# Sliding-window attention and gated FFN on one core: DMA transposes and loads one group earlier, batch 3 on the steady pattern

## The chip, the cores and the metric

The kernel runs on one core of one Trainium2 chip. Times are device microseconds (us) of a whole execution. The kernel before took 365.98 us (median of 6 runs beside the changed one; 365.95 in the three runs from which the prediction starts). The profile's span starts at the first instruction and ends at the last one, and is some 1.75 us shorter than the measured time. Names of engines are those of the profile: PE is TensorE (matmuls), ACT is ScalarE, DVE is VectorE, POOL is GpSimd (here it issues the loads), and SP issues the other transfers from its queue.

## The reference

```python
scores = scale * np.matmul(q, k.transpose(0, 1, 3, 2))      # 8 batches, 8 heads, 576 x 64
mask = (rel >= 0) & (rel < 128)                             # causal window of 128
scores = np.where(mask, scores + bias, -1e9)                # ALiBi bias
attn = softmax(scores)
x = np.matmul(attn, v)  ->  (4608 tokens, 512)
g, val = x @ w_gate, x @ w_val                              # 512 -> 1536
out = (gelu(g) * val) @ w_out                               # 1536 -> 512
```

## The kernel before

The FFN runs in nine groups of 512 tokens. A group is twelve gate blocks (`gate_val`, eight 512-column matmuls each) and eight output halves (`out_half`, six matmuls each). The attention of later batches is woven in between. For each batch there are scores (PE), exps (ACT), a mask product (DVE), row sums (PE), reciprocals (DVE), the spread of the reciprocals over 128 partitions, and values (PE) with a product into `xT` (DVE). The spread is done in two ways: by PE with copies on ACT and DVE, or through DRAM by DMA.

```python
    def transposes_dma(b):                      # q and k of batch b, SBUF to SBUF, on the SP queue
        for src, dst in ((ks, kT), (qs, qT)):
            nc.sync.dma_start_transpose(...)

    def spread_dma(b):                          # 18 KB to DRAM, then two broadcast reads
        d = d_pool.tile([4, 2, S], FP32, name="rd")
        nc.sync.dma_start(out=d.rearrange("c i s -> (c i) s"), in_=sumrow[b][0:128:16, :])
        for i in (0, 1):
            nc.sync.dma_start(out=recip[b][64 * i:64 * i + 64, :, :],
                              in_=d[:, i, :].unsqueeze(0).to_broadcast((64, 4, S)))

    def spread_pe(b, s):                        # four fp32 matmuls (eight records), four copies
        ...

    def finish(b, s):
        spread_pe(b, s)
        values(b, s, range(4))

    todo = {                                    # what stands between the output halves 0 to 7 of a group
        ...
        2: [("s", 3, 1, (0, 1), lambda: sums(3, 0)), 0, ("s", 3, 1, (2, 3)), 1,
            ("finish", 3, 0), ("s2", 4), ("sum", 3, 1), 2,
            ("s", 4, 0, (0, 1)), 3, ("finish", 3, 1), 4, ("s", 4, 0, (2, 3)), 5,
            ("s", 4, 1, (0, 1)), 6, 7, ("s", 4, 1, (2, 3))],
    }
```

`("s", b, s, cs)` is a lot of scores, 8 matmuls where `s` is 0 and 12 where it is 1, into four PSUM banks (PSUM is the memory that takes PE's results; `ps` in the traces). `("s2", b)` is the diagonal block of all heads, two banks. Tiles of PSUM come from eight banks, which are reused in the order in which the program frees them.

The softmax here doesn't subtract the row's maximum and nothing guards it: scores larger than these inputs give would overflow.

Of the kernel before, what the change touches and what calls it, by code (L numbers as in the profile page):

```python
# [26 lines left out]
def kernel(  # L27
# [11 lines left out]
    B, H, S, D = q.shape  # L39
# [27 lines left out]
    def bank():  # L67
        ps = psum.tile([128, 512], FP32, name="ps")
        for _ in range(heat.pop()):
            nc.tensor.matmul(out=ps, lhsT=zeros[:, 0:128], rhs=zeros, start=True, stop=True)  # L70
        heat.append(0)
        return ps
# [19 lines left out]
    def load(t, src, b, js=range(5)):  # L92
        for j in js:
            lo = 64 if j == 0 else 0
            nc.gpsimd.dma_start(  # L95
                out=t[lo:128, j, :].rearrange("p (h d) -> p h d", h=H),
                in_=src[b][:, 128 * j - 64 + lo:128 * j + 64, :].rearrange("h p d -> p h d"))

    def load_qk(b):
        load(qs[b % 2], q, b)  # L100
        load(ks[b % 2], k, b)
# [18 lines left out]
    def load_v(b, js=range(5)):  # L120
        load(vb[b % 2], v, b, js)
# [34 lines left out]
    def transpose(b, what, c, copy):  # L156
        ps = bank().bitcast(BF16)
        for j in range(5):
            nc.tensor.transpose(  # L159
                out=ps[:, 128 * j:128 * j + 128],  # L160
                in_=(qs, ks)[what][b][:, j, 128 * c:128 * c + 128], identity=ident)
        copy(out=(qT, kT)[what][b][:, :, c, :],
             in_=ps[:, 0:640].rearrange("p (j t) -> p j t", t=128))
# [7 lines left out]
    def transposes_dma(b):  # L171
        for src, dst in ((ks, kT), (qs, qT)):
            nc.sync.dma_start_transpose(
                out=dst[b % 2].rearrange("p j c t -> p (j c) t"),
                in_=src[b % 2].rearrange("p j x -> p (j x)"))
# [53 lines left out]
    def prob(b, s, c, i, j, n):  # L229
        if (s, j) == (0, 2):  # L230
            return probs2[b][:, c, i, 0:n]
        return probs[b, s, c][:, i, PCOL[s][j]:PCOL[s][j] + n]
# [3 lines left out]
    def sums(b, s):  # L236

        ps = bank()
        for j, a, e in PIECES[s]:
            for i in (0, 1):  # L240
                for c in range(4):
                    nc.tensor.matmul(  # L242
                        out=ps[32 * c:32 * c + 32, a:e],
                        lhsT=ones[:, min(j, 1), i, :], rhs=prob(b, s, c, i, j, e - a),
                        start=(i == 0 and j == 2 * s), stop=(i == 1 and j == 2 * s + 2),
                        skip_group_check=True)
        if b not in sumrow:
            sumrow[b] = r_pool.tile([128, S], FP32, name="r")
            recip[b] = r_pool.tile([128, 4, S], FP32, name="rb")
        lo, hi = PART[s]  # L250
        nc.vector.reciprocal(sumrow[b][:, lo:hi], ps[:, 0:hi - lo])  # L251

    def spread_dma(b):
# [3 lines that stand above are left out]
            nc.sync.dma_start(  # L257
                out=recip[b][64 * i:64 * i + 64, :, :],
                in_=d[:, i, :].unsqueeze(0).to_broadcast((64, 4, S)))
# [14 lines left out]
    def values(b, s, cs):  # L274
        lo, hi = PART[s]
        pss = []
        for c in cs:
            ps = bank()
            pss.append(ps)
            for j, a, e in PIECES[s]:  # L280
                for i in (0, 1):
                    h = 2 * c + i
                    nc.tensor.matmul(  # L283
                        out=ps[64 * i:64 * i + 64, a:e],
                        lhsT=vb[b % 2][:, j, 64 * h:64 * h + 64],
                        rhs=prob(b, s, c, i, j, e - a),
                        start=(j == 2 * s), stop=(j == 2 * s + 2), skip_group_check=True)
        for c, ps in zip(cs, pss):
            nc.vector.tensor_tensor(  # L289
                out=xT[:, c, b * S + lo:b * S + hi], in0=ps[:, 0:hi - lo],  # L290
                in1=recip[b][:, c, lo:hi], op=ALU.mult)
# [7 lines left out]
    def gate_val(g, f, lo=0, hi=512, later=None):  # L299
        if g not in hid:  # L300
            hid[g] = h_pool.tile([128, NF, 512], BF16, name="hT")
        t0 = 512 * g
        pg, pv = bank(), bank()
        for w, ps in ((wg, pg), (wv, pv)):
            for c in range(4):
                nc.tensor.matmul(  # L306
                    out=ps[:, 0:hi - lo], lhsT=w[:, c, 128 * f:128 * (f + 1)],
                    rhs=xT[:, c, t0 + lo:t0 + hi], start=(c == 0), stop=(c == 3))

        def act():  # L310
            gl = g_pool.tile([128, 512], BF16, name="gelu")
            nc.scalar.activation(out=gl[:, 0:hi - lo], in_=pg[:, 0:hi - lo], func=AF.Gelu)  # L312
            nc.vector.tensor_tensor(out=hid[g][:, f, lo:hi], in0=pv[:, 0:hi - lo],  # L313
                                    in1=gl[:, 0:hi - lo], op=ALU.mult)

        if later is None:
            act()
        else:
            later.append(act)
# [3 lines left out]
    def out_half(g, u):  # L323
        t, half = u // 2, u % 2
        if half == 0:
            acc[g] = bank()
        po = acc[g]
        for f in range(6 * half, 6 * half + 6):
            nc.tensor.matmul(  # L329
                out=po, lhsT=hid[g][:, f, 128 * t:128 * (t + 1)],  # L330
                rhs=wo[:, f, :], start=(f == 0), stop=(f == NF - 1))
        if half == 1:
            osb = o_pool.tile([128, DM], FP32, name="osb")
            nc.scalar.copy(out=osb, in_=po)  # L334
            r0 = 512 * g + 128 * t
            nc.sync.dma_start(out=out[r0:r0 + 128, :], in_=osb)
# [103 lines left out]
    for t in (qs[0], ks[0]):  # L440
# [10 lines left out]
        1: [("s2", 2), ("s", 2, 0, (0, 1)), 0, ("s", 2, 0, (2, 3)), 1, 2,  # L451
            ("s", 2, 1, (0, 1), lambda: sums(2, 0)), 3, ("s", 2, 1, (2, 3)), ("s2", 3),
            ("finish", 2, 0), 4, ("sum", 2, 1), ("s", 3, 0, (0, 1)), 5, 6,
            ("finish", 2, 1), ("s", 3, 0, (2, 3)), 7],
        2: [("s", 3, 1, (0, 1), lambda: sums(3, 0)), 0, ("s", 3, 1, (2, 3)), 1,
            ("finish", 3, 0), ("s2", 4), ("sum", 3, 1), 2,
            ("s", 4, 0, (0, 1)), 3, ("finish", 3, 1), 4, ("s", 4, 0, (2, 3)), 5,
            ("s", 4, 1, (0, 1)), 6, 7, ("s", 4, 1, (2, 3))],
    }

    def steps(g):
        b = g + 2
        if g in todo:
            return todo[g]
        if b >= B:
            return range(8)
        return [("s2", b), ("s", b, 0, (0, 1)), 0, 1, ("s", b, 0, (2, 3)), 2, 3,
                ("s", b, 1, (0, 1)), 4, 5, ("s", b, 1, (2, 3)), 6, 7]

    RUN = {"s2": scores2, "s": scores, "sum": sums, "finish": finish}  # L470

    for g in range(NG):
        for b in ((), (2, 3), (4,))[g] if g < 3 else ():
            transposes_dma(b)
        if g + 2 < B:
            load_v(g + 2)
        for f in range(6 if g == 0 else 0, NF):
            gate_val(g, f)
            if g == 0 and f >= 8:
                for w in (0, 1):  # L480
                    transpose(1, w, f - 8, (act, dve)[w])
            if 3 <= g < B - 1:
                if f == 0:
                    sums(g + 1, 0)
                    sums(g + 1, 1)
                    spread_dma(g + 1)
                    if g + 2 < B:
                        transposes_dma(g + 2)
                elif f in (8, 10):
                    for s in (0, 1):  # L490
                        values(g + 1, s, (f - 8, f - 7))
        if g + 3 < B:
            load_qk(g + 3)
        for item in steps(g):
            if isinstance(item, int):
                out_half(g, item)
            else:
                RUN[item[0]](*item[1:])

# [29 lines left out]
```

## Time and profile before

| | before |
|---|---|
| median time | 365.98 us |
| span of the profile | 364.2 us |
| PE busy | 352.5 us, 97% |
| DVE, ACT busy | 52%, 51% |
| groups 1, 2, 3, 4 | 42.52, 40.21, 37.99, 37.40 us |

The last row is the measure. It is the distance from the first gate row of a group to the first gate row of the next one in the timeline of PE. Groups 4 and 5 have the steady pattern.

### The profile page before, as it was taken

The numbers are of one execution on the slowest core, as the hardware profiler recorded it, in microseconds if no ns is written. First come the engines' busy times: TensorE is split into PE (matmuls) and PEld (weight loads), VectorE is DVE, ScalarE is ACT, GpSimd is POOL, SyncE is SP. The second block draws the span as 40 slices with busy tenths as digits, with TensorE's granted clock in tenths as the row PEclk, the third lists the DMA queues.
The fourth block names the chain that finished last, engine by engine and source line by source line (L and its number), as shares of the span: only waits on it lengthen the run. The fifth ranks groups of instructions, "written<-read, shape, count | busy, mean of one in ns | idle before, by whom it ended". The sixth has DMA issues, their size and how long they took to land.

```text
span 364.2 us, 6748 instructions
## 1 busy us (share of the span) xinstructions
PE 352.5 (97%) x2702; PEld 172.1 (47%) x2702; DVE 189.4 (52%) x308; ACT 187.5 (51%) x340; POOL 109.1 (30%) x140
## 2 busy tenths in 40 slices
PE   7899999999999999999999999999999999999995
PEld 2467545444454445444444444444444444444442
DVE  4876458533795369484537554745465404302320
ACT  5963486435956376933883278336842223313321
POOL 8966769912629103900940040000000000000000
PEclk9999999999999999999999999999999999999999
DMA  9999999999979985999991992093205030011002
GB/s 105 161 193 175 172 161 185 183 147 193 178 100 131 153 67 83 164 101 218 117 213 42 199 112 88 35 200 71 88 33 130 2 115 0 4 58 58 2 29 86
DMA packets 151168, 41.41 MB, mean 114 GB/s; under 512 B 138816, under 2 KB 144448, under 8 KB 151136
## 3 DMA queue, kind: packets, MB, share of 16 engines
q0 software_dynamic: 112608, 18.88, 67.9%
q1 hardware_dynamic: 38528, 22.10, 27.7%
q8 instruction: 21, 0.34, 0.4%
q14 instruction: 11, 0.09, 0.1%
HBM read 42.47 MB, written 9.51 MB: 143 GB/s over the span
## 4 chain that ended last, share of the span: by engine, by line
PE 86%; ACT 5%; DMA 2%; POOL 2%; DVE 2%; issue 1%; POOLq 0%; DVEq 0%; ACTq 0%
PE ps L306 51%; PE ps L329 24%; PE ps L283 4%; ACT P L187 4%; PE ps L180 3%; DMA vb<-in_v_dram 2%; PE ps L242 2%; PE ps L265 1%; DVE xT L289 1%; ACT L187 1%; POOL ks L115 1%; DVE P L190 1%; PE ps L159 1%; POOL qs L115 1%; DVE r L251 0%
## 5 line engine op out<-in xcount | busy, mean ns | idle before, releaser
L313 DVE TENSOR_TENSOR hT<-ps,gelu 128x512 bf16<-128x512 f32 (+2 forms) x114 | 74.4, 659 | 119.7 <-PE ps L306 104.7
L312 ACT ACTIVATE gelu<-ps 128x512 bf16<-128x512 f32 (+2 forms) x114 | 65.2, 575 | 117.1 <-PE ps L306 115.8
L306 PE MATMUL ps<-xT,wg 128*128 128x512 bf16 (+2 forms) x456 | 112.7, 368 | 0.7 <-DVE xT L289 0.4
L306 PE MATMUL ps<-xT,wv 128*128 128x512 bf16 (+2 forms) x456 | 111.9, 368 | 0.0
L329 PE MATMUL ps<-wo,hT 128*128 128x512 bf16 x432 | 99.1, 380 | 0.0
L187 ACT ACTIVATE P<-ps 128x512 bf16<-128x512 f32 x144 | 74.3, 629 | 9.3 <-PE ps L180 9.3
L306 PEld LDWEIGHTS <-wv 128*128 128x128 bf16 x456 | 44.3, 98 | 49.5 <-issue 0.5
L306 PEld LDWEIGHTS <-wg 128*128 128x128 bf16 x456 | 43.0, 98 | 47.9 <-issue 1.2
L190 DVE TENSOR_TENSOR P<-P,emask 128x1024 bf16<-128x1024 bf16 x72 | 48.6, 690 | 30.1 <-ACT P L187 29.8
L329 PEld LDWEIGHTS <-hT 128*128 128x128 bf16 x432 | 39.7, 98 | 49.0 <-issue 4.4
L95 POOL DMA_DIRECT2D vb<-in_v_dram x40 | 33.8, 869 | 72.9 <-PE ps L283 72.7
L334 ACT COPY osb<-ps 128x512 f32<-128x512 f32 x36 | 21.7, 602 | 36.9 <-PE ps L329 32.5
L95 POOL DMA_DIRECT2D qs<-in_q_dram x35 | 29.7, 878 | 24.9 <-DMA qT<-qs 14.6
L251 DVE RECIPROCAL r<-ps 128x320 f32<-128x320 f32 (+1 forms) x16 | 30.7, 1937 | 3.0 <-PE ps L242 3.0
L95 POOL DMA_DIRECT2D ks<-in_k_dram x35 | 29.6, 887 | 6.0 <-DMA qs<-in_q_dram 3.6
L289 DVE TENSOR_TENSOR xT<-ps,rb 128x320 bf16<-128x320 f32 (+1 forms) x64 | 24.6, 446 | 1.6 <-PE ps L283 1.0
L180 PE MATMUL ps<-qT,kT 64*128 64x256 bf16 (+1 forms) x384 | 22.6, 245 | 1.8 <-DVE kT L149 1.0
L180 PEld LDWEIGHTS <-kT 64*128 64x128 bf16 x384 | 12.8, 94 | 15.7 <-issue 11.4
L283 PE MATMUL ps<-P,vb 128*64 128x128 bf16 (+2 forms) x384 | 18.9, 244 | 1.1 <-DMA vb<-in_v_dram 1.0
L283 PEld LDWEIGHTS <-vb 128*64 128x64 bf16 x384 | 14.8, 109 | 8.2 <-issue 6.4
L242 PE MATMUL ps<-P,ones 128*32 128x128 bf16 (+2 forms) x384 | 10.5, 243 | 1.1 <-DVE P L190 1.1
L242 PEld LDWEIGHTS <-ones 128*32 128x32 bf16 x384 | 7.8, 96 | 5.3 <-issue 4.2
(50 smaller groups left out, 96.6 us busy)
## 6 DMA issues: line engine op xcount, KB each, us to landing
out_dram<-osb SPq DMA_DIRECT2D x36, 256.0 KB, 3.3
rb<-rd SPq DMA_DIRECT2D x8, 576.0 KB, 7.1
vb<-in_v_dram POOLq DMA_DIRECT2D x32, 128.0 KB, 5.7
qs<-in_q_dram POOLq DMA_DIRECT2D x28, 128.0 KB, 5.9
ks<-in_k_dram POOLq DMA_DIRECT2D x28, 128.0 KB, 5.9
wg<-in_moe_w_gate_dram POOLq DMA_DIRECT2D x4, 384.0 KB, 8.8
wv<-in_moe_w_val_dram POOLq DMA_DIRECT2D x4, 384.0 KB, 9.9
wo<-in_moe_w_out_dram POOLq DMA_DIRECT2D x2, 768.0 KB, 11.2
```

What stands on the lines that cost most here:

```text
L95: nc.gpsimd.dma_start(out=t[lo:128, j, :].rearrange("p (h d) -> p h d", h=H), in_=src[b][:, 128 * j - 64 + lo:128 * j + 64, :].rearrange(" ...
L180: nc.tensor.matmul(out=ps[:, col:col + 128 * n].rearrange("p (n t) -> p n t", n=n), lhsT=blocks(kT, b, i, c, j, 1).rearrange("p n t -> p ( ...
L187: nc.scalar.activation(out=dst, in_=src, func=AF.Exp, scale=0.125)
L190: nc.vector.tensor_tensor(out=dst, in0=dst, in1=m, op=ALU.mult)
L242: nc.tensor.matmul(out=ps[32 * c:32 * c + 32, a:e], lhsT=ones[:, min(j, 1), i, :], rhs=prob(b, s, c, i, j, e - a), start=(i == 0 and j == ...
L251: nc.vector.reciprocal(sumrow[b][:, lo:hi], ps[:, 0:hi - lo])
L283: nc.tensor.matmul(out=ps[64 * i:64 * i + 64, a:e], lhsT=vb[b % 2][:, j, 64 * h:64 * h + 64], rhs=prob(b, s, c, i, j, e - a), start=(j == ...
L289: nc.vector.tensor_tensor(out=xT[:, c, b * S + lo:b * S + hi], in0=ps[:, 0:hi - lo], in1=recip[b][:, c, lo:hi], op=ALU.mult)
L306: nc.tensor.matmul(out=ps[:, 0:hi - lo], lhsT=w[:, c, 128 * f:128 * (f + 1)], rhs=xT[:, c, t0 + lo:t0 + hi], start=(c == 0), stop=(c == 3))
L312: nc.scalar.activation(out=gl[:, 0:hi - lo], in_=pg[:, 0:hi - lo], func=AF.Gelu)
L313: nc.vector.tensor_tensor(out=hid[g][:, f, lo:hi], in0=pv[:, 0:hi - lo], in1=gl[:, 0:hi - lo], op=ALU.mult)
L329: nc.tensor.matmul(out=po, lhsT=hid[g][:, f, 128 * t:128 * (t + 1)], rhs=wo[:, f, :], start=(f == 0), stop=(f == NF - 1))
```

## The change

The changed kernel wants batch 3 to run like the later batches. Its last scores move to the end of group 1, its sums into the first two gate blocks of group 2, and its reciprocals go through DRAM. Its values stand between the output halves of group 2. The DMA transposes and the loads of q and k go one group further ahead. In group 2 the last scores of batch 4 now stand before the last output half.

```diff
--- before.py
+++ after.py
@@ -451,11 +451,11 @@
         1: [("s2", 2), ("s", 2, 0, (0, 1)), 0, ("s", 2, 0, (2, 3)), 1, 2,
             ("s", 2, 1, (0, 1), lambda: sums(2, 0)), 3, ("s", 2, 1, (2, 3)), ("s2", 3),
             ("finish", 2, 0), 4, ("sum", 2, 1), ("s", 3, 0, (0, 1)), 5, 6,
-            ("finish", 2, 1), ("s", 3, 0, (2, 3)), 7],
-        2: [("s", 3, 1, (0, 1), lambda: sums(3, 0)), 0, ("s", 3, 1, (2, 3)), 1,
-            ("finish", 3, 0), ("s2", 4), ("sum", 3, 1), 2,
-            ("s", 4, 0, (0, 1)), 3, ("finish", 3, 1), 4, ("s", 4, 0, (2, 3)), 5,
-            ("s", 4, 1, (0, 1)), 6, 7, ("s", 4, 1, (2, 3))],
+            ("finish", 2, 1), ("s", 3, 0, (2, 3)), 7, ("s", 3, 1, (0, 1)),
+            ("s", 3, 1, (2, 3))],
+        2: [("s2", 4), ("s", 4, 0, (0, 1)), 0, 1, ("s", 4, 0, (2, 3)), 2, 3,
+            ("pv", 3, 0, (0, 1)), ("pv", 3, 1, (0, 1)), 4, ("s", 4, 1, (0, 1)), 5,
+            ("pv", 3, 0, (2, 3)), ("pv", 3, 1, (2, 3)), 6, ("s", 4, 1, (2, 3)), 7],
     }
 
     def steps(g):
@@ -467,7 +467,7 @@
         return [("s2", b), ("s", b, 0, (0, 1)), 0, 1, ("s", b, 0, (2, 3)), 2, 3,
                 ("s", b, 1, (0, 1)), 4, 5, ("s", b, 1, (2, 3)), 6, 7]
 
-    RUN = {"s2": scores2, "s": scores, "sum": sums, "finish": finish}
+    RUN = {"s2": scores2, "s": scores, "sum": sums, "finish": finish, "pv": values}
 
     for g in range(NG):
         for b in ((), (2, 3), (4,))[g] if g < 3 else ():
@@ -479,18 +479,20 @@
             if g == 0 and f >= 8:
                 for w in (0, 1):
                     transpose(1, w, f - 8, (act, dve)[w])
-            if 3 <= g < B - 1:
+            if 2 <= g < B - 1:
                 if f == 0:
                     sums(g + 1, 0)
+                if f == (1 if g == 2 else 0):
                     sums(g + 1, 1)
                     spread_dma(g + 1)
-                    if g + 2 < B:
-                        transposes_dma(g + 2)
-                elif f in (8, 10):
+                    if g + 3 < B:
+                        transposes_dma(g + 3)
+                elif g > 2 and f in (8, 10):
                     for s in (0, 1):
                         values(g + 1, s, (f - 8, f - 7))
-        if g + 3 < B:
-            load_qk(g + 3)
+        for b in ((3,), (4, 5))[g] if g < 2 else (g + 4,):
+            if b < B:
+                load_qk(b)
         for item in steps(g):
             if isinstance(item, int):
                 out_half(g, item)
```

## The prediction

> **What bounds the kernel now.** I read the page first (parts 1, 2 and 4), then the waits of PE, then the timelines of PE and ACT around the group boundaries, then the DMA issues and the SP queue's timeline.
>
> ```profile
> span 364.2 us, 6748 instructions
> ...
> PE 352.5 (97%) x2702; PEld 172.1 (47%) x2702; DVE 189.4 (52%) x308; ACT 187.5 (51%) x340; POOL 109.1 (30%) x140
> ...
> PE   7899999999999999999999999999999999999995
> ...
> DMA  9999999999979985999991992093205030011002
> ...
> PE 86%; ACT 5%; DMA 2%; POOL 2%; DVE 2%; issue 1%; POOLq 0%; DVEq 0%; ACTq 0%
> ```
>
> The reader is to see that PE has work in 352.5 of 364.2 us and that 86% of the chain that ended last is PE. The other 11.7 us are the start (the windows give 25.35 us busy in the first 30.5), the last output write (about 3.9 us after the last matmul), and small gaps. So only PE work that disappears, or a PE gap that opens or closes, can move the time. DMA is busy for two thirds of the span, but the waits of PE name a DMA only four times, for 1.7 us in all, everything before 20 us. The loads of q and k that the change moves are nowhere on the path.
>
> The boundary between groups 1 and 2, in the timelines of PE and ACT (start, duration):
>
> ```profile
> 106.89 0.71 PE L265 MATMUL ps<-r,sel 32*128 32x256 f32 x8
> 107.54 1.07 PE L283 MATMUL ps<-P,vb 128*64 128x128 bf16 x24
> 108.54 0.64 PE L180 MATMUL ps<-qT,kT 64*128 64x256 bf16 x8
> 109.11 1.47 PE L329 MATMUL ps<-wo,hT 128*128 128x512 bf16 x6
> 110.42 1.03 PE L306 MATMUL ps<-xT,wg 128*128 128x512 bf16 x4
> ```
>
> ```profile
> 108.97 2.06 ACT L187 ACTIVATE P<-ps 128x512 bf16<-128x512 f32 x4 [0.70 <-PE ps L180]
> 110.90 0.62 ACT L334 COPY osb<-ps 128x512 f32<-128x512 f32 x1
> 111.53 1.28 ACT L312 ACT_TABLE_LOAD   x1
> 112.82 1.09 ACT L312 ACTIVATE gelu<-ps 128x512 bf16<-128x512 f32 x2
> ```
>
> PE runs through the boundary without a gap, ACT is about one microsecond behind it. The boundary between groups 2 and 3 has a gap:
>
> ```profile
> 150.08 0.61 PE L180 MATMUL ps<-qT,kT 64*128 64x128 bf16 x12
> 150.63 1.04 PE L306 MATMUL ps<-xT,wg 128*128 128x512 bf16 x4
> 151.50 1.03 PE L306 MATMUL ps<-xT,wv 128*128 128x512 bf16 x4
> 152.46 0.73 PE L242 MATMUL ps<-P,ones 128*32 128x192 bf16 x27
> 153.57 0.60 PE L242 MATMUL ps<-P,ones 128*32 128x128 bf16 x21 [0.37 <-DVE P L190]
> ```
>
> Here the last scores of batch 4 are the last thing in group 2, and the sums at the start of group 3 wait for their exps and mask.
>
> **What the skill says.** The Trainium skill, "TensorE: Matmul & The Clock Gate", section "Back-to-back issue gap", gives N / 2.4 + 2.5 ns for an isolated warm matmul, 216 ns at 512 columns. The trace agrees: four gate matmuls start 0.86 to 0.87 us after the four before, 216 ns each, though the duration column says 380. So I count PE time by differences of start times, never by durations. "ScalarE: Activation LUTs", section "What ACT_TABLE_LOAD costs", gives 186 ns + 0.833 N for an ACTIVATE with immediate scale, back-to-back ones overlapping by about 93 ns: 520 ns each at 512. The trace has 2.06 us for four exps, 515 each, and 1.28 us for a table load. "Perfetto Trace Analysis", section "Optimizing Tensor Performance", wants matmul groups to rotate through PSUM banks so that evacuation overlaps; the term below where PE outruns ACT is exactly this. "DMA: Bandwidth & Descriptors", section "Issuing engines are not separate DMA queues", says that all issuers share the same 16 engines: earlier loads add no bandwidth, they only begin elsewhere. The trace shows busy engines until some 115 us, then pauses.
>
> **The change part by part.**
>
> (a) *Batch 3 no longer spreads its reciprocals on PE.* Both finish items of group 2 go; with them two PE spreads and their eight copies (four on ACT, four on DVE, about 0.4 to 0.5 us each, beside PE). A spread costs PE the distance from its start to that of the values behind it: 135.74 to 136.49 is 0.75 us, 141.84 to 142.49 is 0.65 us. Sum 1.40 us of PE. In their place stand one write and two reads through DRAM on the SP queue, no PE work.
>
> (b) *The rest of batch 3 moves, it is not removed.* Its last scores (24 matmuls, 0.55 us twice) go to the end of group 1; its sums (48 matmuls) go into the first two gate blocks of group 2; its values (96 matmuls) go between the output blocks. As a check I take whole groups from the first gate row of each: group 2 lasts 110.42 to 150.63, 40.21 us; group 4, which already has the steady pattern, lasts 188.62 to 226.02, 37.40 us. The new group 2 has just the work of group 4, with its sums in two places instead of one. Each change of matmul kind in a 512-column stream costs about 0.1 us (six output matmuls take 1.40 us between other work, 1.30 by 216 ns). So 37.50. From the 40.21 I subtract 37.50 and the 1.20 that goes to group 1 (two times 0.55 and a break): **1.5 us saved**, which agrees with (a).
>
> (c) *The end of group 2.* The last scores of batch 4 now stand one output item (1.4 us) before the end. The mask for the sums of batch 4 was 0.37 us late, now it is early. Group 3 lasts 150.63 to 188.62, 37.99 us, against 37.40 for group 4, so this can give back up to **0.6 us**.
>
> (d) *The end of group 1.* Three lots of scores (12 exps, 6.2 us of ACT at 515 ns, plus an output copy) now meet some 3 us of PE work. The eight PSUM banks go round in the order in which the program frees them. The exps of the lot at 108.54 free banks at about 109.5, 110.0, 110.5 and 111.0, the output copy at 111.5. The first moved lot takes three banks of the values (their DVE products ended at 109.75) and the first of these: no wait. The second takes the other three and the output's bank: it reaches that one at about 111.3 and waits to 111.57, **0.3 us**. Its own successors on ACT: exps of the first moved lot end at 112.0, 112.5, 113.0, 113.55, of the second at 114.1 to 115.6. The first gate block of group 2 wants a bank at 111.85 and gets it at 112.05: **0.2 us**. The second sums of batch 3 want the last mask (115.6 + 0.7, ready about 116.35) at 116.1: **0.3 us**. The first gelu then comes at 116.9 (a table load after the last exp) and its product on DVE is done at 118.2; the fourth gate block wants these banks at 118.7: no wait, but by half a microsecond only. The two reciprocals of batch 3 (2.16 and 1.74 us on DVE) lie between the first gate products; by my count they end at 122.8, just where the sixth gate block needs the bank: up to 0.3 us, more likely nothing. Loss here **0.8 us**.
>
> (e) *Transposes and loads one group ahead.* PE waited for neither. The transposes of batch 4 start at 112.10 in the SP queue as before and land by about 125; their scores now begin some 134, instead of 137.6: slack shrinks but stays. The reciprocals of batch 3 go to DRAM and back behind them, issued at about 125 to 128, 7.1 us to land, so there at about 136; the first product that reads them comes at about 141. Loads of batch 5 start when the transposes of batch 3 have read the buffers (about 94), in a stretch around 105 to 112 where DMA paused. Worth **0**.
>
> Sum: -1.5 - 0.6 + 0.8 = -1.3 us, so 365.95 - 1.3 = **364.6 us**.
>
> **The rivals.**
>
> 1. *A new wait at the end of group 1 takes all the gain.* For it: ACT is behind by half a microsecond of slack in the gate blocks after, and the DVE chain (masks, products, two reciprocals) is in order. If one more round of banks comes late, some 1 to 2 us are lost: 365.5 to 366.5. Against: before, the gelu started 3.5 us after the first gate block of group 3 with two reciprocals behind it, and PE did not wait again after the sums; now it would be 4.9 us.
>
> 2. *DMA is the hidden bound and the loads were late.* Then more distance would pay by several microseconds, towards 362. Against: no PE wait names a transpose, and the groups from 4 on, with transposes one group ahead, show no gap at all.
>
> 3. *The SP queue jams in group 2.* Four transposes and the spread sit in order before the output writes of group 2; the transposes keep the queue 4 to 8 us each. If the first output write goes only after 145, the fourth copy to the three output buffers is late and holds ACT: 1 to 3 us lost, 366 to 367. Against: I place the queue free at 139 to 142, the fourth copy at 149.
>
> **Range and chances.** The removed PE work (1.4) is sure. Rivals 1 and 3 take up to 2 or 3 us, with a quarter of the weight together; rival 2 or fewer bank waits give 0.8 more. Runs of before scatter by 0.5. So 363.6 to 366.0. The 2% band is 7.3 us on either side, and nothing in sight reaches it: faster 0.01, within 97 in 100, slower 0.02.
>
> **What would show it.** Right: spread matmuls of L265 down from 64 to 48 and PE's busy time down by about 1.4 (durations overlap, so not exactly); the distance between the first gate rows of groups 2 and 3 about 37.5 to 38.3; group 3 about 37.4 with no wait for a mask; small waits for ACT in the scores and gates around 111 to 112 and for a mask near 116. Wrong: a PE gap above 1 us anywhere between 110 and 125; a wait for the spread-back reciprocals or for qT and kT near 134 to 141; a changed length of groups 4 and later, where nothing should move.

## More of the kernel before

One profile was taken of each kernel, so a length of a group is that of one execution.

PE hardly ever stands still, so a group's length is its PE work plus its waits, and it does not depend on how the start of the run went.

## The result, and the profile after

| | before | after |
|---|---|---|
| median of 6 runs | 365.98 us | 364.46 us (363.84 to 364.78) |
| span of the profile | 364.2 us | 362.8 us |
| group 1 | 42.52 us | 44.17 us |
| group 2 | 40.21 us | 37.61 us |
| group 3 | 37.99 us | 37.40 us |
| group 4 | 37.40 us | 37.40 us |

The ratio is 0.9948, with a 95% interval of 0.9927 to 0.9969. A ratio here is the mean time of one kernel's fast runs over that of the other's of the same rounds, so it is not quite the ratio of the medians. Executions over 1.5% slower than the fastest of the same kernel are left out of the means. The time is within 2%, and the change is faster by a small, clear amount. The three changed groups give +1.65, -2.60 and -0.59, together -1.54 us. In the two profiles the start was 0.34 us later and the stretch from group 5 on about 0.2 us shorter, which gives the 1.4 us between the spans.

The page of the changed kernel, the same parts as before:

```profile
span 362.8 us, 6665 instructions
...
PE 349.6 (96%) x2642; PEld 172.5 (48%) x2686; DVE 187.7 (52%) x304; ACT 186.3 (51%) x336; POOL 108.9 (30%) x140
...
DMA  9999999999999999999921992150206030011002
...
PE 86%; ACT 5%; DMA 3%; POOL 2%; DVE 2%; issue 2%; POOLq 0%; DVEq 0%; ACTq 0%
```

PE still carries 86% of the chain. The fall of PE's busy time by 2.9 us is too large to be read as work removed: this trace lacks some matmul records (2642 against 2686 weight loads). The spread matmuls of L265 fell from 64 to 48. In slices 12 to 16 of the 40 (100 to 146 us) the DMA row read 7, 9, 9, 8, 5 before and reads 9 throughout now: the loads of batch 5 (issued from 97.4 us on, before from 111.4), those of batch 6 (from 122.7) and the transposes of batch 5 (from 127.3) fill the gaps.

The end of group 1 in the timeline of PE (start, duration), with the two moved lots of scores at 110.86 to 112.41:

```profile
108.89 0.64 PE L180 MATMUL ps<-qT,kT 64*128 64x256 bf16 x8
109.69 1.24 PE L329 MATMUL ps<-wo,hT 128*128 128x512 bf16 x5 [0.16 <-issue]
110.86 0.89 PE L180 MATMUL ps<-qT,kT 64*128 64x128 bf16 x19
111.91 0.38 PE L180 MATMUL ps<-qT,kT 64*128 64x128 bf16 x5 [0.16 <-ACT osb L334]
112.41 1.02 PE L306 MATMUL ps<-xT,wg 128*128 128x512 bf16 x4
```

```profile
111.24 0.62 ACT L334 COPY osb<-ps 128x512 f32<-128x512 f32 x1
111.71 4.08 ACT L187 ACTIVATE P<-ps 128x512 bf16<-128x512 f32 x8
115.81 1.28 ACT L312 ACT_TABLE_LOAD   x1
117.10 1.80 ACT L312 ACTIVATE gelu<-ps 128x512 bf16<-128x512 f32 x3
```

The second block is the timeline of ACT. The row of the output half lacks its first matmul record (`x5`); it began at about 109.46, so it took 1.40 us, the break to the scores included. Two lots without a wait would take 1.10 us, so the gate would start at 111.96; it starts at 112.41. Of these 0.45 us the profile names 0.16, the wait for the bank of the last output copy; the rest lies before the first gate matmul and has no name. ACT does the eight exps of the moved lots first (111.71 to 115.79) and reaches the first gelu 4.7 us after the first gate row.

The boundary of groups 2 and 3, where the kernel before waited for a mask:

```profile
148.17 0.62 PE L180 MATMUL ps<-qT,kT 64*128 64x128 bf16 x12
148.72 1.47 PE L329 MATMUL ps<-wo,hT 128*128 128x512 bf16 x5
150.02 1.03 PE L306 MATMUL ps<-xT,wg 128*128 128x512 bf16 x4
150.89 1.03 PE L306 MATMUL ps<-xT,wv 128*128 128x512 bf16 x4
151.84 1.12 PE L242 MATMUL ps<-P,ones 128*32 128x192 bf16 x48
```

All 48 sums are in one row without a gap. The last scores stand one output half earlier.

The SP queue in group 2 of the changed kernel (start and duration of the issue):

```profile
112.44 4.58 SPq L173 DMA_TRANSPOSE kT<-ks  x1
117.20 3.69 SPq L173 DMA_TRANSPOSE qT<-qs  x1
122.72 0.71 SPq L255 DMA_DIRECT2D rd<-r  x1
125.76 1.32 SPq L257 DMA_DIRECT2D rb<-rd  x2
127.30 9.95 SPq L173 DMA_TRANSPOSE kT<-ks  x1
137.42 6.92 SPq L173 DMA_TRANSPOSE qT<-qs  x1
144.43 7.08 SPq L336 DMA_DIRECT2D out_dram<-osb  x4
```

The four transposes and the spread stand in order before the first output write of the group, which goes at 144.43 us.

### The profile page after: what moved, and what is told of

It is laid out like the page before. It is cut to its first block, busy times and chain, and to the rows that moved or that the text cites. A ratio compares the mean times of both kernels' runs of the same rounds, so it can differ in the third digit from the quotient of the medians.

```text
span 362.8 us, 6665 instructions
## 1 busy us (share of the span) xinstructions
PE 349.6 (96%) x2642; PEld 172.5 (48%) x2686; DVE 187.7 (52%) x304; ACT 186.3 (51%) x336; POOL 108.9 (30%) x140
## 4 chain that ended last, share of the span: by engine, by line
PE 86%; ACT 5%; DMA 3%; POOL 2%; DVE 2%; issue 2%; POOLq 0%; DVEq 0%; ACTq 0%
PE ps L306 51%; PE ps L329 23%; PE ps L283 4%; ACT P L187 4%; PE ps L180 3%; DMA vb<-in_v_dram 3%; PE ps L242 2%; DVE xT L289 1%; PE ps L265 1%; ACT L187 1%; POOL ks L115 1%; PE ps L159 1%; POOL qs L115 1%; DVE r L251 0%; POOL vb L95 0%
## 5 line engine op out<-in xcount | busy, mean ns | idle before, releaser
L306 PE MATMUL ps<-xT,wg 128*128 128x512 bf16 (+2 forms) x441 | 110.9, 368 | 1.4 <-DVE xT L289 0.4
L329 PE MATMUL ps<-wo,hT 128*128 128x512 bf16 x413 | 97.1, 380 | 1.5 <-issue 0.8
```

What stands on the lines that cost most here:

```text
L306: nc.tensor.matmul(out=ps[:, 0:hi - lo], lhsT=w[:, c, 128 * f:128 * (f + 1)], rhs=xT[:, c, t0 + lo:t0 + hi], start=(c == 0), stop=(c == 3))
L329: nc.tensor.matmul(out=po, lhsT=hid[g][:, f, 128 * t:128 * (t + 1)], rhs=wo[:, f, :], start=(f == 0), stop=(f == NF - 1))
```

## The experiments

My theory: the gain is PE work taken away (the spread of batch 3) and a mask that is no longer late, less the waits at the end of group 1; the distance of the loads is worth nothing. Rivals: the distance is what pays; or the gain is from waits alone. All results were correct. The whole times of the first four kernels were taken on a chip where the kernel before itself scattered from 365.35 to 369.0 us.

| kernel | group 1 | group 2 | group 3 | group 4 | sum |
|---|---|---|---|---|---|
| before | 42.52 | 40.21 | 37.99 | 37.40 | 158.12 |
| changed | 44.17 | 37.61 | 37.40 | 37.40 | 156.58 |
| e1 schedule only | 44.16 | 37.61 | 37.61 | 37.39 | 156.77 |
| e2 ahead only | 42.52 | 40.21 | 37.99 | 37.40 | 158.12 |
| e3 PE spread | 44.16 | 39.12 | 37.39 | 37.40 | 158.07 |
| e4 old tail | 44.16 | 37.61 | 38.03 | 37.40 | 157.20 |
| e5 tail only | 42.51 | 40.23 | 37.39 | 37.40 | 157.53 |
| e6 scores apart | 44.73 | 37.63 | 37.40 | 37.39 | 157.15 |
| e7 relief | 43.37 | 37.61 | 38.47 | 37.40 | 156.85 |
| e8 relief, apart | 43.64 | 37.63 | 37.39 | 37.40 | 156.06 |
| e9 relief, late values | 43.36 | 37.61 | 37.50 | 37.40 | 155.87 |
| e10 relief, old distance | 43.36 | 37.61 | 37.88 | 37.40 | 156.25 |
| e11 changed again | 44.17 | 37.61 | 37.70 | 37.39 | 156.87 |
| e12 relief, held loads | 43.35 | 37.62 | 37.39 | 37.39 | 155.75 |

### e1: the order of work alone

```diff
 (against the changed kernel)
-                    if g + 3 < B:
-                        transposes_dma(g + 3)
+                    if g > 2 and g + 2 < B:
+                        transposes_dma(g + 2)
-        for b in ((3,), (4, 5))[g] if g < 2 else (g + 4,):
-            if b < B:
-                load_qk(b)
+        if g + 3 < B:
+            load_qk(g + 3)
```

> The changed order of the work in groups 1 and 2 and the DMA spread of batch 3's reciprocals, but loads and DMA transposes at the old distance. My theory (PE work removed, DMA distance worth nothing): the same as the changed kernel, 364.2 to 364.8 us, some 1.4 us under the kernel before; first gate rows of groups 2, 3 and 4 37.6 and 37.4 us apart. Rival (the loads ahead are what pays): 365.5 to 366.

The profiled run took 364.52 us; the time as a whole missed the expectation and was unclear (366.96 us median of all six, the slow one included; ratio 0.9985, interval 0.9948 to 1.0022). By the groups the new order alone gives 1.35 of the 1.54 us. Group 3 is 0.2 us longer than in the changed kernel: its scores of batch 5 begin just where the transposes of batch 5 land. The trace names no cause for that gap, so e10 tries it again. (DVE's wait for the read-back of the reciprocals, which e7 and e11 below make a rival, was only 1.5 us here, less than in the changed kernel.)

### e2: the distance alone

```diff
 (against the kernel before)
-                    if g + 2 < B:
-                        transposes_dma(g + 2)
+                    if g + 3 < B:
+                        transposes_dma(g + 3)
-        if g + 3 < B:
-            load_qk(g + 3)
+        for b in ((3,), (4, 5))[g] if g < 2 else (g + 4,):
+            if b < B:
+                load_qk(b)
         for item in steps(g):
             ...
+        if g == 2:
+            transposes_dma(5)
```

> The old order of the work, with the loads of q and k one group further ahead and the DMA transposes too from group 3 on (those of batch 5 are issued after the steps of group 2, because its buffers are read until then). My theory: no change against the kernel before, within 0.3 us of 366. Rival (loads ahead pay): about 364.5. Second rival (they cost by contention, and the order pays more than it shows): over 366.5.

365.94 us, and all four groups as before to 0.01 us. In the old order the distance is worth nothing.

### e3: batch 3 spread on PE again

```diff
 (against the changed kernel)
-        2: [("s2", 4), ("s", 4, 0, (0, 1)), 0, 1, ("s", 4, 0, (2, 3)), 2, 3,
+        2: [("s2", 4), ("s", 4, 0, (0, 1)), 0, 1, ("s", 4, 0, (2, 3)), 2, ("spread", 3, 0), 3,
+            ("spread", 3, 1),
-                    spread_dma(g + 1)
+                    if g > 2:
+                        spread_dma(g + 1)
```

> The changed kernel with batch 3's reciprocals spread by PE again, in group 2 between output halves 2 and 3 and after 3. My theory: the removed PE work comes back whole, 1.4 us and two breaks of 0.1, so 365.8 to 366.3; group 2 gets 1.4 to 1.9 us longer, all else alike. Rival (the gain is from shorter waits, not from the PE work): under 365.

366.02 us; its profiled run has the span of the kernel before, 364.2 us. Only group 2 changed, by 1.51 us. The timeline of PE shows what came back:

```profile
139.75 0.82 PE L265 MATMUL ps<-r,sel 32*128 32x320 f32 x8
140.50 1.47 PE L329 MATMUL ps<-wo,hT 128*128 128x512 bf16 x6
141.90 0.71 PE L265 MATMUL ps<-r,sel 32*128 32x256 f32 x8
142.55 1.13 PE L283 MATMUL ps<-P,vb 128*64 128x192 bf16 x24
```

The spreads take 0.75 and 0.65 us from start to start, as before the change; the rest, 0.11 us, is a break between kinds of matmul.

### e4 and e5: the end of group 2

```diff
 (e4, against the changed kernel)
-            ("pv", 3, 0, (2, 3)), ("pv", 3, 1, (2, 3)), 6, ("s", 4, 1, (2, 3)), 7],
+            ("pv", 3, 0, (2, 3)), ("pv", 3, 1, (2, 3)), 6, 7, ("s", 4, 1, (2, 3))],
 (e5, against the kernel before)
-            ("s", 4, 1, (0, 1)), 6, 7, ("s", 4, 1, (2, 3))],
+            ("s", 4, 1, (0, 1)), 6, ("s", 4, 1, (2, 3)), 7],
```

> The changed kernel with the old end of group 2 (both last output halves, then the last scores of batch 4). My theory: the mask of batch 4 is late again for the sums in group 3, which gets 0.4 to 0.6 us longer (37.8 to 38.0 instead of 37.4): 364.9 to 365.1. Rival (that wait was noise or came from DVE's load before): no change, 364.5.

> The kernel before with one thing changed: in group 2 the last scores of batch 4 stand before the last output half, not after it. My theory: the 0.37 us wait for the mask at the start of group 3 goes, group 3 lasts 37.4 to 37.6 us instead of 37.99, all other groups are as before; span 363.6 to 363.9. Rival (the mask is late because of DVE's reciprocals, not because of the place of the scores): group 3 stays at 38.0.

e4 took 365.56 us (ratio 0.9965, interval 0.9934 to 0.9995; more than the 364.9 to 365.1 expected, on the scattering chip) and lost 0.63 us in group 3; the wait for the mask is back in PE's timeline:

```profile
151.63 0.73 PE L242 MATMUL ps<-P,ones 128*32 128x192 bf16 x27
152.78 0.60 PE L242 MATMUL ps<-P,ones 128*32 128x128 bf16 x21 [0.42 <-DVE P L190]
```

e5 took 365.31 us (ratio 0.9975, interval 0.9958 to 0.9992) and gained 0.60 us in group 3, with nothing else moved. One swap of two items is worth 0.6 us from either side, whatever else is in the kernel.

### e6: the last scores of group 1 set apart

```diff
 (against the changed kernel)
-            ("finish", 2, 0), 4, ("sum", 2, 1), ("s", 3, 0, (0, 1)), 5, 6,
-            ("finish", 2, 1), ("s", 3, 0, (2, 3)), 7, ("s", 3, 1, (0, 1)),
-            ("s", 3, 1, (2, 3))],
+            ("finish", 2, 0), 4, ("sum", 2, 1), ("s", 3, 0, (0, 1)), 5, ("s", 3, 0, (2, 3)), 6,
+            ("finish", 2, 1), ("s", 3, 1, (0, 1)), 7, ("s", 3, 1, (2, 3))],
```

> The changed kernel with the three last lots of scores of group 1 set apart by output halves and the finish of batch 2 (lot, half, finish, lot, half, lot). My theory (PE outruns ACT there and waits for banks): the two waits of some 0.5 us between the last output half of group 1 and the first gate of group 2 shrink to 0.2 or less, group 1 lasts 43.6 to 43.9 instead of 44.17. Rival (those 0.5 us are the cost of switching between kinds of matmul): no change.

365.04 us: a miss. Group 1 lasted 44.73 us instead of less. 0.31 us of it is a wait for the transposes of batch 2 at the start of the steps, before the edit. The rest moved: the scores behind the finish of batch 2 now waited 0.39 us for banks that DVE's copies of the spread held. Set apart in this way, the wait moved from ACT's banks to DVE's and grew; e7 shows that another order does remove a wait in these steps.

### e7 and e8: a wait in the middle of group 1

Both kernels have an older wait in group 1: the first spread of batch 2 and its values run stretched, right behind a lot and a diagonal block of scores whose exps ACT has not done (in the changed kernel PE begins the spread at 98.99 us, and ACT is at these exps until 101.6). In the changed kernel the two rows took 1.46 and 1.59 us from start to start; in e7 they took 0.75 and 1.14.

```diff
 (e7, against the changed kernel)
-            ("s", 2, 1, (0, 1), lambda: sums(2, 0)), 3, ("s", 2, 1, (2, 3)), ("s2", 3),
-            ("finish", 2, 0), 4, ("sum", 2, 1), ("s", 3, 0, (0, 1)), 5, 6,
+            ("s", 2, 1, (0, 1), lambda: sums(2, 0)), 3, ("s", 2, 1, (2, 3)), 4,
+            ("finish", 2, 0), ("s2", 3), ("sum", 2, 1), ("s", 3, 0, (0, 1)), 5, 6,
```

> The changed kernel with the first half of the spread of batch 2 one output half later and the third kind of scores of batch 3 (the diagonal block) behind it. The trace shows the spread and values there stretched by 1.2 us against their like later in the group, as their banks wait for ACT's exps. My theory: most of that is recovered, group 1 43.0 to 43.4 us instead of 44.17. Rival (ACT has no room in these steps, so the wait moves to another place in group 1 or the start of group 2): groups 1 and 2 together stay at 81.8.

> Both of the last two together. My theory: the gains add, group 1 lasts 42.6 to 43.0 us and the span is 361.2 to 361.8, which would beat both kernels. Rival (as ACT is the bound of these steps): no better than the better of the two alone.

e7 took 363.66 us (ratio 0.9925, interval 0.9908 to 0.9941), e8, with the edits of e6 and e7, 363.5 us (0.9929, 0.9908 to 0.9950). In e7 group 1 fell by 0.80 us to 43.37, as expected. In e8 it lasted 43.64, where 42.6 to 43.0 was expected: a miss, the two edits do not add. But e7 lost 1.07 us in group 3, where nothing was edited. The timelines of PE and of DVE there:

```profile
169.00 1.03 PE L306 MATMUL ps<-xT,wv 128*128 128x512 bf16 x4
170.67 1.47 PE L283 MATMUL ps<-P,vb 128*64 128x192 bf16 x24 [0.65 <-DVE xT L289]
```

```profile
165.51 0.69 DVE L313 TENSOR_TENSOR hT<-ps,gelu 128x512 bf16<-128x512 f32 x1 [1.03 <-PE ps L306]
170.13 1.55 DVE L289 TENSOR_TENSOR xT<-ps,rb 128x320 bf16<-128x320 f32 x4 [3.92 <-PE ps L306]
```

DVE stood still for 3.9 us before the products of batch 4, although their matmuls (at 165.34) were long done. The profile puts that to PE, the releaser that came last by its count; the other operand is the reciprocals, which come back through DRAM. The issue of the read-back had slipped to 161.43, 4.9 us after the write's issue at 156.51. In the changed kernel DVE's wait there was 2.7 us, named as one for that DMA, and PE lost nothing. e8 has the same order of work in group 3 and also lost nothing: there the read-back was issued 4.1 us after the write and DVE waited 1.9 us. So the loss goes with the length of this round trip, which varies, and not with e7's edit as such. e7's profiled run was also the slowest of its four (364.16 us, the others 363.44 to 363.71), so the others may have lost less; no profile shows them.

### e9 and e10: later values, and the distance once more

```diff
 (e9, against e7)
-                elif g > 2 and f in (8, 10):
+                elif g > 2 and f in ((9, 11) if g == 3 else (8, 10)):
                     for s in (0, 1):
-                        values(g + 1, s, (f - 8, f - 7))
+                        c = 2 * (f > 9)
+                        values(g + 1, s, (c, c + 1))
 (e10, against e9: the edit of e1)
```

> The relieved group 1 (first spread of batch 2 one output half later), and in group 3 the two groups of values of batch 4 one gate block later (behind blocks 9 and 11), as there the read-back of the reciprocals came 3.9 us late for DVE and cost PE 1.1 us. My theory (that read-back is the cause): group 3 is back at 37.4 to 37.5 us, group 1 stays at 43.4, group 2 at 37.6: span some 361.2 to 361.6, 1.3 us under the changed kernel on the same chip. Rival (DVE is late in group 3 for another reason): group 3 stays at 38 or more.

> The same with loads and transposes at the old distance. In the schedule-only kernel group 3 was 0.2 us longer, with the scores of batch 5 beginning just where the transposes of batch 5 should land. My theory (with the shorter group 2 the old distance has no slack left): group 3 lasts 37.6 to 37.9 us, all other groups as in the kernel beside it; so the distance is worth 0.2 to 0.5 us there, not zero. Rival (that 0.2 us was chance): 37.4, no difference.

e9 took 363.73 us (ratio 0.9939, interval 0.9909 to 0.9969); its profiled run was the one with the late start. Group 3 was back at 37.50 us. e10 took 364.9 us (0.9967, 0.9940 to 0.9993), with group 3 at 37.88 and every other group equal. Here PE's timeline names the cause:

```profile
173.12 0.84 PE L180 MATMUL ps<-qT,kT 64*128 64x128 bf16 x16 [0.52 <-DMA qT<-qs]
```

So in the new order the old distance is too short by 0.2 (e1) to 0.4 us (e10 against e9): the scores of batch 5 wait for its transposes. These stand behind the read-back in the SP queue, so they were late from two sides: the scores come 0.6 us earlier in the group, and the transposes landed later in it (24.3 us into group 3 in e1 and 24.6 in e10, where the kernel before has 24.0).

### e11: the changed kernel again

The edit is none.

> The changed kernel again, for comparison on this chip: groups 1 to 4 at 44.2, 37.6, 37.4 and 37.4 us, 1.2 to 1.7 us under the kernel before in time.

364.75 us (ratio 0.9958, interval 0.9933 to 0.9983). Groups 1, 2 and 4 repeat to 0.01 us, but group 3 lasted 37.70 instead of 37.40: DVE's wait for the read-back was 3.1 us this time:

```profile
170.85 1.55 DVE L289 TENSOR_TENSOR xT<-ps,rb 128x320 bf16<-128x320 f32 x4 [3.15 <-DMA rb<-rd]
```

PE's values beside it took 0.28 us longer than in the other profile of the same kernel; the profile names no releaser for that. With e7 and e8 this gives a scale: 1.9 and 2.7 us of DVE's wait cost PE nothing, 3.1 us went with 0.3, 3.9 us with 1.07. The changed kernel stands at the edge.

### e12: the loads held back in group 3

```diff
 (against e7)
+    hold = consts.tile([128, 1], FP32, name="hold")
         ...
-        if g + 2 < B:
+        if g + 2 < B and g != 3:
             load_v(g + 2)
         ...
                     spread_dma(g + 1)
+                    if g == 3:
+                        nc.gpsimd.tensor_copy(out=hold, in_=recip[4][:, 0, 0:1])
+                        load_v(5)
```

> The relieved group 1 as in the relief kernel, values of batch 4 at their old place, but in group 3 the loads of v for batch 5 and of q and k for batch 7 are held until the reciprocals of batch 4 have been read back (a one-column copy on GpSimd reads them first). My theory (the loads in flight slow the write and the read-back of the reciprocals, which then hold DVE, banks and PE): the gap from the write's issue to the reads' issue falls from 4.9 us to about 2, DVE waits under 1 us for the read-back, and group 3 lasts 37.4 instead of 38.47 us; span 361.2 to 361.6 if the start is a usual one. Rival (the round trip itself is slow there, loads or not): gap over 4 us and group 3 at 38 or more.

363.4 us (363.19 to 363.87; ratio 0.9923, interval 0.9903 to 0.9943). Group 3 lasts 37.39 us and DVE's wait for the read-back is gone from the list of waits. The write and the read-back in the SP queue, in the repeated changed kernel and then in this one:

```profile
157.50 0.62 SPq L255 DMA_DIRECT2D rd<-r  x1
162.49 1.26 SPq L257 DMA_DIRECT2D rb<-rd  x2
```

```profile
156.78 0.62 SPq L255 DMA_DIRECT2D rd<-r  x1
158.65 1.26 SPq L257 DMA_DIRECT2D rb<-rd  x2
```

The gap falls from 4.99 to 1.87 us when the loads of v, q and k are not in flight beside it. In the ten other profiles with the new order it was 3.5 to 5.0 us, and in the three with the old order (before, e2, e5) 1.86 to 1.88, so this is no chance of one run. The span of its profile, 362.1 us, was longer than expected (361.2 to 361.6), in part because this profiled run began its group 1 at 68.36 us, e7's at 67.57. By its groups this is the shortest of all kernels here, 0.83 us under the changed kernel and 2.37 under the one before. The 1.08 us that group 3 gains on e7 is the gain on e7's slowest run: by the medians of their times e12 and e7 differ by 0.26 us, on two chips, and the intervals of their ratios overlap nearly whole. By time, it is under the kernel before with a clear interval. Against the changed kernel it ran on another chip, and the two ratios' intervals overlap.

## Why the prediction was right

The time (364.46 us against 364.6) was right, and for most of its reasons. That it came within 0.2 us is in part luck: group 3 of the same kernel varies by 0.3 us (e11), and the start by more. By its own steps:

- **Step (a) and (b), the spread and what moves.** Right. The predicted saving was 1.5 us, and e3 gave 1.51 back. Group 2 was to last 37.5 and lasted 37.61: two rows of 24 sums take 0.61 and 0.56 us from start to start, where group 4's one row of 48 takes 1.05, so the second place cost 0.1 us more than the one break that was counted. (The values of a batch are 48 matmuls, not 96; the sum did not use that number.)
- **Step (c), the end of group 2.** Right: 0.6 us predicted, 0.59 measured, 0.63 and 0.60 by e4 and e5.
- **Step (d), the end of group 1.** Two of its three terms hold, the third did not occur. Group 1 was to grow by 1.2 and two waits of 0.3 and 0.2 us, 1.7 in all, and grew by 1.65: 1.2 and waits of 0.45. Allowing for the later start of 0.34 us, the bank of the output copy came when the arithmetic said. The 0.3 us for the mask of the second sums did not arise: the mask was done at 116.51, the sums began at 116.67. PE came 0.2 us later than counted, and the mask earlier. So the loss was about 0.5 us, not 0.8; less the 0.1 us by which group 2 was longer than 37.5, that is the 0.2 us by which the groups (-1.54 us) beat the forecast of -1.3.
- **Step (e), the distance of transposes and loads.** "Worth 0" holds for the old order alone (e2). In the new order it is worth 0.2 to 0.4 us: without it the scores of batch 5 wait (e1, e10). I compared PE's waits of the kernel before, in which the steps of group 3 begin 24.9 us into the group. I did not ask where they would begin when (c) had shortened it: 24.3 us, at the very time the transposes land in e1.
- **Not in the prediction: the read-back of batch 4 in group 3.** I followed the reciprocals of batch 3 through the SP queue but not those of batch 4. Batch 3's last values now stand later in group 2 (145.71 us instead of 142.49), so GpSimd's loads start later (those of v at 146.5 us instead of 137.8 and 143.7), run beside that round trip, and stretch it (e12). In the run of the result it cost nothing, in e11 0.3 us.
- **Rival 1** (a new wait takes all the gain) fell, with the margin that step (d) gave. **Rival 2** (DMA is the hidden bound) fell as a cause of the gain, but holds in small as (e) shows. **Rival 3** (the SP queue jams): I placed the queue free at 139 to 142 us; the first output write went at 144.43, 0.6 us from the point I had named as the one where it hurts. The fourth copy came at 150.53, not at 149, and did not wait. This was nearer than argued: the transposes of batch 5 held the queue for 9.95 and 6.92 us, beside the loads of batch 6. The prediction also read the DMA row wrongly: it has the engines busy until some 115 us and paused after, but the row dips at 100 to 109 us and at 127 to 146, and is full in between.

What stays open is the start: the first gate row of group 1 moves by a microsecond or more between kernels whose order of work up to there is the same (67.57 us in e7, 70.47 in e9), as much as this change is worth. No experiment here went into it.

## What to carry to other kernels

When one engine is busy in nearly all of the span, count a change by that engine's start-to-start times in whole sections, and compare a section with another that already has the new form; that gave the saving here to 0.1 us. A transfer for which no engine waits may still be close to late: when the order of work gets shorter, ask again where each transfer lands and who then reads it. Bulk loads that nobody needs soon can be held back until a small round trip on the path is done; in group 3 that was worth 1.1 us in the one run where the round trip was slow enough to hold PE so long (e7), and 0 to 0.3 us by the two profiles of the changed kernel.

## What the Trainium skill lacked or had wrong

- "TensorE: Matmul & The Clock Gate", section "Back-to-back issue gap": it gives 131 ns per matmul as the sustained spacing at 512 columns in a stream of weight loads and matmuls, and 216 ns for the isolated one. In this stream, which has just that form, the spacing is 216 ns (four matmuls in 0.86 to 0.87 us, group after group).
- "ScalarE: Activation LUTs", section "What ACT_TABLE_LOAD costs": it adds a drain of about 1.38 us to the load of 1.28 us. Here a switch costs the load alone: the exps before it end at 115.79, the load runs from 115.81 to 117.09 and the gelu starts at 117.10.
- "DMA: Bandwidth & Descriptors", section "Latency and other measured facts": it has a lighter fixed cost for a lighter HBM load, but no figure for a small write and its dependent read beside bulk loads. Here the gap from issue to issue was 1.87 us with the loads held back and 3.5 to 5.0 us beside them, in group 3.
- On no page that I read: how long it takes to put another kind of matmul into a stream of 512-column ones ("TensorEngine Tiling (Array Packing)", section "Key Properties", says that a change of the tiling mode drains TensorE, with no time). Here six output matmuls take 1.40 us between other work and 1.30 by their spacing, so 0.1 us for each break.
